# Two groups' scores in one row-tiled session, projections out of the attention's banks, and a re-ordered opening, in a sliding-window attention followed by a SwiGLU block

## The chip, the cores and the metric

One core of one Trainium2 chip. The metric is device time in microseconds (us) of one execution; the trace is taken on one such execution, and its span is 1.6 to 2 us shorter than the device time of that same execution. Engines: PE is TensorE's matmuls, PEld its weight loads, DVE is VectorE, ACT is ScalarE, POOL is GpSimd, SP is the engine whose queue issues all the DMAs here. "Faster" or "slower" needs 2%.

## The reference

Causal attention with a window of 64 positions, 8 batches x 8 heads x 576 positions x 64, then a SwiGLU feed-forward block over 4608 tokens (512 to 1536 to 512):

```python
scores = (1/8) * q @ k.T                  # masked to 0 <= i - j < 64
attn = exp(scores - max); attn = attn / (sum(attn) + 1e-9)
x = (attn @ v) as [4608, 512]
g = x @ w_gate;  h = g * (1 / (1 + exp(-g))) * (x @ w_val)
out = h @ w_out                           # float32 in and out
```

## The kernel before

Tokens go through in 36 groups of 128 (attention) and 9 tiles of 512 (feed-forward). Everything is cast to bf16 and multiplied there. The parts that matter here:

```python
ps_a: 3 banks of PSUM   # scores, products, transposes, in rotation
ps_f: 2 x 2 banks       # gate and value of a feed-forward step
ps_o: 1 bank            # projection, and the warm-up matmuls

def scores(g):                     # one "session": 16 matmuls of 64 rows
    ps = [ps_a.tile(...) for _ in range(2)]
    for b in range(2):
        for p in range(4):
            for a in range(2):
                nc.tensor.matmul(ps[a][:, p, 1 - b], kT[...], qT[...], tile_position=(64 * a, 0))
    for a in range(2):
        act.activation(e, ps[a][:], AF.Exp, scale=0.125)
        dve.tensor_mul(e, e, mask)             # both inputs in SBUF, bf16

def products(g):                   # 16 matmuls of 65 columns, then on DVE:
    ...                            # reciprocal and multiply, twice, from PSUM

def step(t, m):                    # 4 gate and 4 value matmuls, 128x512 each, Tanh on ACT,
    ...                            # then on DVE the two operations of the PREVIOUS step
                                   # ("finish"), which free its gate and value banks

def warm(n):                       # n matmuls of zeros, to keep TensorE active
    for _ in range(n): nc.tensor.matmul(w_ps[:], wz[:, 0:P], wz[:])

# opening: a long fixed list of calls. It loads and transposes k and q, does the
# attention of groups 0 to 11 and the scores of 12, all of tile 0 and the gate/value
# steps of tile 1, while the weights arrive. Then the loop:
for w in range(8, 36):
    t, s = divmod(w, 4)
    step(t, 3 * s)
    products(w + 4)
    ...                            # casts of k, q and v on POOL
    step(t, 3 * s + 1)
    scores(w + 5)
    turn_x1(w + 4)                 # DMA transpose of the group's x, for tile t + 1
    step(t, 3 * s + 2)
    ...                            # DMA transposes of k or q
    project(t - 1, s)              # 12 matmuls 128x512, out by ACT and DMA
    ...                            # next loads
for s in range(4): project(8, s)
```

The softmax here doesn't subtract the row's maximum and nothing guards it: scores larger than these inputs give would overflow.

## Time and profile before

| | before |
|---|---|
| device time, median | 355.39 us (3 runs, 354.25 to 355.47) |
| span of the trace | 352.3 us |
| first feed-forward matmul | 27.32 us |
| start of the loop (first step of tile 2) | 97.63 us |
| last matmul ends | 348.45 us |

The page's busy table and its slices of the span (each digit is a tenth of busy time, or of full clock, in one fortieth of the span; GB/s is what DMA moved):

```profile
PE 336.3 (95%) x2629; PEld 164.3 (47%) x2629; DVE 232.4 (66%) x488; ACT 149.2 (42%) x255; POOL 101.3 (29%) x144
...
PEclk9999999999999999999999999999999999999999
...
GB/s 205 241 283 298 308 248 285 283 203 153 99 169 183 158 164 180 165 158 159 179 152 178 158 171 163 168 151 180 151 181 165 106 74 47 45 60 33 30 60 89
```

PE is busy 95% of the span, but that hides two stages. The loop is bound by PE. Here is one loop step in the timeline of PE (start, duration, what, count; the products between are left out). Durations overlap because matmuls are pipelined, so starts are what to read:

```profile
204.75 1.03 PE L258 MATMUL g_ps<-xT,wg 128*128 128x512 bf16 x4
205.62 1.03 PE L258 MATMUL v_ps<-xT,wv 128*128 128x512 bf16 x4
206.58 0.41 PE L176 MATMUL s_ps<-qT,kT 64*128 64x64 bf16 x16
206.92 1.04 PE L258 MATMUL g_ps<-xT,wg 128*128 128x512 bf16 x4
...
213.45 1.02 PE L258 MATMUL g_ps<-xT,wg 128*128 128x512 bf16 x4
```

Four 128x512 matmuls take 0.865 us from start to start (205.62 minus 204.75, which the lines show rounded), 0.216 each. A step with products and scores takes 213.45 minus 204.75 = 8.70 us, one without both 7.77. The session sits between the value matmuls and the next gate matmuls: 206.92 - 205.62 - 0.865 = 0.43 us. The 16 scores start 14.5 ns apart, so 0.21 us of that is not score work but entering and leaving.

The opening is different. From the durations, its 71.6 us of PE work (24 steps x 1.727, 4 projections x 2.59, 12 products x 0.48, 13 sessions x 0.44, transposes) take 97.6 us. PE's waits between 27 and 98 us, longest first (total us, times, longest), and pieces of the chain of waits in the same stretch (start, us, what):

```profile
PE s_ps L176 <- ACT E L182: 2.5, 2, 2.2
PE tp L141 <- POOL q_fb L110: 1.6, 1, 1.6
PE tp L141 <- DVE k_fb L110: 0.5, 1, 0.5
```

```profile
23.03 3.06 SPq L235
...
30.67 6.22 DMA w_f<-in_moe_w_val_dram
...
53.55 9.70 DMA k_f<-in_k_dram
...
73.58 5.45 DMA q_f<-in_q_dram
```

PE waits little after 27 us; the chain goes through the DMA queue and single loads (a weight block, then k and q).

### The profile page before, as it was taken

To read this page: it belongs to the slowest core of one execution; us is meant where nothing else is said; L and a number is where in the kernel's file an instruction comes from. 1 tells how busy PE (TensorE), PEld (TensorE's weight loads), DVE (VectorE), ACT (ScalarE), POOL (GpSimd) and SP (SyncE) were. 2 spreads that over 40 slices of the span, in tenths; PEclk is the share of its full clock that TensorE was granted. 3 is DMA by queue.
4 is the path that set the end of the run, shared out by engine and by line. 5 is a ranking of instruction groups with operands and counts; after the bars stand their busy time and mean duration, and the time that the engine had idled before them with its cause. 6 is when DMAs were issued, how large, how long until landed. Compare 5 with 4: busy or idle time off the path is not lost.

```text
span 352.3 us, 6919 instructions
## 1 busy us (share of the span) xinstructions
PE 336.3 (95%) x2629; PEld 164.3 (47%) x2629; DVE 232.4 (66%) x488; ACT 149.2 (42%) x255; POOL 101.3 (29%) x144
## 2 busy tenths in 40 slices
PE   8679989997999999999999999999999999999995
PEld 3445544454544444444444444444444444444442
DVE  4778988765786766676667666666666676555510
ACT  2557853649443333333333333333333333333221
POOL 1755445420214324232324151515061310000000
PEclk9999999999999999999999999999999999999999
DMA  8999999997379788989999988888798431110012
GB/s 205 241 283 298 308 248 285 283 203 153 99 169 183 158 164 180 165 158 159 179 152 178 158 171 163 168 151 180 151 181 165 106 74 47 45 60 33 30 60 89
DMA packets 152417, 57.08 MB, mean 162 GB/s; under 512 B 127808, under 2 KB 146240, under 8 KB 152384
## 3 DMA queue, kind: packets, MB, share of 16 engines
q1 hardware_dynamic: 152384, 56.64, 76.1%
q8 instruction: 20, 0.33, 0.4%
q14 instruction: 13, 0.11, 0.1%
HBM read 37.75 MB, written 9.44 MB: 134 GB/s over the span
## 4 chain that ended last, share of the span: by engine, by line
PE 77%; DMA 8%; SPq 8%; DVE 4%; ACT 2%; issue 1%; DVEq 0%; ACTq 0%
PE o_ps L275 24%; PE g_ps L258 22%; PE v_ps L258 21%; SPq L235 3%; DMA k_f<-in_k_dram 3%; PE s_ps L176 3%; PE ao_ps L198 2%; PE ao_ps L202 2%; DMA w_f<-in_moe_w_val_dram 2%; SPq L82 2%; PE w_ps L287 2%; DMA q_f<-in_q_dram 2%; DMA xT<-x_b 1%; SPq L93 1%; DVE hT L270 1%
## 5 line engine op out<-in xcount | busy, mean ns | idle before, releaser
L258 PE MATMUL g_ps<-xT,wg 128*128 128x512 bf16 x432 | 111.1, 380 | 0.5 <-DMA xT<-x_b 0.3
L258 PE MATMUL v_ps<-xT,wv 128*128 128x512 bf16 x432 | 110.9, 379 | 0.1
L275 PE MATMUL o_ps<-wo,hT 128*128 128x512 bf16 x432 | 98.5, 379 | 0.0
L263 ACT ACTIVATE th<-g_ps 128x512 f32<-128x512 f32 x108 | 64.6, 599 | 67.0 <-PE g_ps L258 65.8
L269 DVE SCALAR_TENSOR_TENSOR sg<-th,g_ps 128x512 f32<-128x512 f32 x108 | 73.5, 681 | 15.8 <-ACT th L263 15.7
L270 DVE TENSOR_TENSOR hT<-sg,v_ps 128x512 bf16<-128x512 f32 x108 | 74.3, 688 | 9.4 <-DVE sg L269 0.5
L258 PEld LDWEIGHTS <-wv 128*128 128x128 bf16 x432 | 42.0, 98 | 51.5 <-POOL wv L110 0.6
L275 PEld LDWEIGHTS <-hT 128*128 128x128 bf16 x432 | 42.0, 98 | 50.1
L258 PEld LDWEIGHTS <-wg 128*128 128x128 bf16 x432 | 37.8, 98 | 39.0 <-DMA xT<-x_b 1.7
L183 DVE TENSOR_TENSOR E<-E,mask 128x512 bf16<-128x512 bf16 x72 | 34.9, 492 | 22.1 <-ACT E L182 20.4
L182 ACT ACTIVATE E<-s_ps 128x512 bf16<-128x512 f32 x72 | 39.0, 595 | 18.8 <-PE s_ps L176 18.8
L206 DVE RECIPROCAL r<-ao_ps 128x4 f32<-128x4 f32 x72 | 12.7, 177 | 45.2 <-PE ao_ps L202 45.2
L110 POOL CAST ve<-v_f 64x512 bf16<-64x512 f32 x65 | 40.8, 628 | 4.0
L110 POOL CAST q_fb<-q_f 128x1024 bf16<-128x1024 f32 x12 | 12.5, 1038 | 71.0 <-DMA q_f<-in_q_dram 64.7
L207 DVE TENSOR_TENSOR x_b<-ao_ps,r 128x256 bf16<-128x256 f32 x72 | 30.6, 425 | 2.5
L110 POOL CAST k_fb<-k_f 128x1024 bf16<-128x1024 f32 (+1 forms) x14 | 14.4, 1030 | 61.8 <-DMA k_f<-in_k_dram 53.3
L110 POOL CAST vo<-v_f 128x512 bf16<-128x512 f32 x33 | 20.7, 627 | 37.8 <-DMA v_f<-in_v_dram 34.8
L198 PE MATMUL ao_ps<-ve,E 128*128 128x65 bf16 x288 | 22.8, 193 | 3.1 <-DVE x_b L207 1.2
L198 PEld LDWEIGHTS <-E 128*128 128x128 bf16 x288 | 20.1, 97 | 7.0 <-DVE x_b L207 1.9
L202 PE MATMUL ao_ps<-vo,E 128*128 128x65 bf16 x288 | 22.9, 193 | 0.0
L202 PEld LDWEIGHTS <-E 128*128 128x128 bf16 x288 | 18.9, 97 | 4.2 <-issue 0.5
L176 PEld LDWEIGHTS <-kT 64*128 64x128 bf16 x576 | 11.0, 95 | 19.1 <-issue 16.3
(84 smaller groups left out, 138.4 us busy)
## 6 DMA issues: line engine op xcount, KB each, us to landing
v_f<-in_v_dram SPq DMA_DIRECT2D x32, 256.0 KB, 4.5
q_f<-in_q_dram SPq DMA_DIRECT2D x23, 256.0 KB, 4.5
k_f<-in_k_dram SPq DMA_DIRECT2D x23, 256.0 KB, 4.1
w_f<-in_moe_w_val_dram SPq DMA_DIRECT2D x6, 512.0 KB, 8.0
w_f<-in_moe_w_gate_dram SPq DMA_DIRECT2D x6, 512.0 KB, 7.6
wo_f<-in_moe_w_out_dram SPq DMA_DIRECT2D x6, 512.0 KB, 8.0
k_f<-in_k_dram SPq DMA_DIRECT2D x4, 512.0 KB, 7.4
q_f<-in_q_dram SPq DMA_DIRECT2D x4, 512.0 KB, 6.8
```

The source lines that it names most:

```text
L110: eng.tensor_copy(y, x)
L176: nc.tensor.matmul(ps[a][:, p, 1 - b], kT[g // 2 % KR][y, p, o:o + P], qT[g // 2 % QR][y, p, o:o + 64], tile_position=(64 * a, 0),)
L182: act.activation(e, ps[a][:], AF.Exp, scale=0.125)
L183: dve.tensor_mul(e, e, mk[:].unsqueeze(1).to_broadcast([P, 4, 2, 64]))
L198: nc.tensor.matmul(o_ps[:, i, :], E[:, e + P:e + 2 * P], ve[g % VR][:, y, :], start=True, stop=False,)
L202: nc.tensor.matmul(o_ps[:, i, :], E[:, e:e + P], vo[g % VR][:, y, :], start=False, stop=True,)
L207: dve.tensor_mul(x_b[:, 256 * h:256 * h + 256].rearrange("r (y d) -> r y d", y=4), o_ps[:, :, 0:D], r[:].unsqueeze(2).to_broadcast([P, 4, D]),
L258: nc.tensor.matmul(ps[:, 0:n], w[:, c, P * m:P * m + P], xT[t][:, c, c0:c0 + n], start=(c == 0), stop=(c == 3),)
L263: act.activation(th[:, 0:n], g_ps[:, 0:n], AF.Tanh, scale=0.5)
L269: dve.scalar_tensor_tensor(sg[:, 0:n], th[:, 0:n], 1.0, g_ps[:, 0:n], ALU.add, ALU.mult)
L270: dve.tensor_mul(hT[t][:, m, c0:c0 + n], sg[:, 0:n], v_ps[:, 0:n])
L275: nc.tensor.matmul(o_ps[:], hT[t][:, c, P * s:P * s + P], wo[:, c, :], start=(c == 0), stop=(c == 11),)
```

## The change

The intent: one change of TensorE's tiling mode for two groups instead of for one; four shared banks to hold two groups' scores, won by giving up the projection's own bank; and a new order of the opening, with helpers that can split the cast of v over engines.

```diff
-    ps_a = ... tc.tile_pool(name="ps_a", bufs=3, space=PSUM)
+    ps_a = ... tc.tile_pool(name="ps_a", bufs=4, space=PSUM)
-    ps_o = ... tc.tile_pool(name="ps_o", bufs=1, space=PSUM)
...
 def scores(g):        # the matmuls only
+    sps[g] = ps
+def weigh(g):         # Exp and mask
+    for a, x in enumerate(sps.pop(g)): ...
...
-    def project(t, s, ps=None, tag="o"):    # and warm(): from ps_a now
+    def project(t, s):
...
     (the opening: the same calls in a new order; loads start k1, q0, k0, q1; scores(5), (4), (6)
      in one session before the first step; one step of tile 0 in two halves; scores up to 13)
...
         step(t, 3 * s + 1)
-        if w + 5 < NG:
-            scores(w + 5)
+        if odd:
+            for g in range(w + 5, min(w + 7, NG)):
+                scores(g)
+            if w + 5 < NG:
+                weigh(w + 5)
         turn_x1(w + 4)
         step(t, 3 * s + 2)
+        if odd and w + 6 < NG:
+            weigh(w + 6)
```

The rewriting of `finish` changes no order: it still follows one step behind.

More of the change, by code (lines that the diff above doesn't have):

```diff
@@ L45 @@
     hpool = ctx.enter_context(tc.tile_pool(name="hpool", bufs=2))
-    ps_a = ctx.enter_context(tc.tile_pool(name="ps_a", bufs=3, space=PSUM))
+    ps_a = ctx.enter_context(tc.tile_pool(name="ps_a", bufs=4, space=PSUM))
     ps_f = ctx.enter_context(tc.tile_pool(name="ps_f", bufs=2, space=PSUM))
-    ps_o = ctx.enter_context(tc.tile_pool(name="ps_o", bufs=1, space=PSUM))
     wg = cst.tile([P, 4, DFF], BF16, name="wg")
@@ L150, in turn2, with cast_v @@
             copy(eng, y, x)
-    def cast_v(g, eng, parts=(0, 1, 2)):
+    def cast_v(g, engs):
         x = staged["v_f", g // 2][:, g % 2]
         lo, hi = slice(0, 64), slice(64, P)
-        for i in parts:
-            if i == 0:
-                copy(eng, vo[g % VR][:, :, 0:D], x)
-            if i == 1:
-                copy(eng, ve[g % VR][hi, :, 0:D], x[lo])
-            if i == 2 and g + 1 < NG:
-                copy(eng, ve[(g + 1) % VR][lo, :, 0:D], x[hi])
-    def scores(g):
-        E = Es[g % ER]
-        mk = masks[0]
-        for b in range(2):
-            if (2 * g + b) % 9 == 0:
-                mk = masks[2 - b]
+        engs = engs if isinstance(engs, tuple) else (engs,) * 3
+        z = vo[g % VR]
+        copy(engs[0], z[:, :, 0:D], x)
+        for e, a, b in ((engs[1], ve[g % VR][hi], lo), (engs[2], ve[(g + 1) % VR][lo], hi)):
+            if e is None:
+                dve.tensor_copy(a, z[b])
+            else:
+                copy(e, a[:, :, 0:D], x[b])
+    sps = {}
+    def scores(g):
         ps = [ps_a.tile([P, 4, 2, 64], FP32, name="s_ps", tag="a") for _ in range(2)]
@@ L179, in scores @@
                     )
-        for a in range(2):
+        sps[g] = ps
+    def weigh(g):
+        E = Es[g % ER]
+        mk = masks[0]
+        for b in range(2):
+            if (2 * g + b) % 9 == 0:
+                mk = masks[2 - b]
+        for a, x in enumerate(sps.pop(g)):
             e = E[:, 1:25].rearrange("r (h y) x -> r h y x", y=3)[:, a:H:2, 0:2, :]
-            act.activation(e, ps[a][:], AF.Exp, scale=0.125)
+            act.activation(e, x[:], AF.Exp, scale=0.125)
             dve.tensor_mul(e, e, mk[:].unsqueeze(1).to_broadcast([P, 4, 2, 64]))
@@ L249, with step @@
     hT = {}
-    def gv(t, m, c0=0, n=512):
+    pend = []
+    def step(t, m, c0=0, n=512):
         if t not in hT:
@@ L263, in gv, with finish @@
         act.activation(th[:, 0:n], g_ps[:, 0:n], AF.Tanh, scale=0.5)
-        return g_ps, v_ps, th, t, m, c0, n
-    def finish(state):
-        g_ps, v_ps, th, t, m, c0, n = state
+        pend.append((g_ps, v_ps, th, t, m, c0, n))
+    def finish():
+        g_ps, v_ps, th, t, m, c0, n = pend.pop(0)
         sg = fsb.tile([P, 512], FP32, name="sg", tag="sg")
@@ L270, in finish @@
         dve.tensor_mul(hT[t][:, m, c0:c0 + n], sg[:, 0:n], v_ps[:, 0:n])
-    def project(t, s, ps=None, tag="o"):
-        o_ps = (ps or ps_o).tile([P, 512], FP32, name="o_ps", tag=tag)
+    def project(t, s):
+        o_ps = ps_a.tile([P, 512], FP32, name="o_ps", tag="a")
         for c in range(12):
@@ L284, in warm @@
     def warm(n):
-        w_ps = ps_o.tile([P, 512], FP32, name="w_ps", tag="o")
+        w_ps = ps_a.tile([P, 512], FP32, name="w_ps", tag="a")
         for _ in range(n):
             nc.tensor.matmul(w_ps[:], wz[:, 0:P], wz[:])
-    pend = None
-    def step(t, m, c0=0, n=512):
-        nonlocal pend
-        st = gv(t, m, c0, n)
-        if pend:
-            finish(pend)
-        pend = st
-    def flush():
-        nonlocal pend
-        finish(pend)
-        pend = None
     def begin():
@@ L327 @@
     begin()
+    load(1, k, "k_f")
+    load(0, q, "q_f")
     load(0, k, "k_f")
-    load(0, q, "q_f")
-    load_vg(0)
-    cast_k(0, "k_f", dve)
-    warm(18)
-    turn2(0, "k_f", act)
-    load(1, k, "k_f")
-    keys_before(1)
-    cast_k(0, "q_f", (dve, act))
-    load(1, q, "q_f")
-    load_vg(1)
-    warm(5)
-    turn2(0, "q_f", (dve, act))
-    cast_k(1, "k_f", pool)
-    cast_k(1, "q_f", dve)
+    load(1, q, "q_f")
+    cast_k(0, "k_f", (act, pool))
+    cast_k(0, "q_f", dve)
+    warm(11)
@@ L343 @@
+    turn2(0, "q_f", (dve, act))
+    load_vg(0)
     cast_v(0, pool)
     load_vg(2)
+    cast_v(2, pool)
+    cast_k(1, "k_f", (dve, act))
+    warm(3)
+    turn2(0, "k_f", (dve, act))
+    load_vg(1)
+    cast_k(1, "q_f", dve)
+    turn2(1, "k_f", (dve, act))
+    keys_before(1)
+    warm(1)
+    turn2(1, "q_f", (dve, act))
+    scores(1)
+    weigh(1)
+    load(2, q, "q_f")
+    warm(1)
+    scores(0)
+    weigh(0)
+    warm(1)
+    scores(2)
+    weigh(2)
     cast_v(1, pool)
+    cast_k(2, "q_f", (dve, act))
@@ L346 @@
+    load(3, k, "k_f")
+    warm(5)
+    products(0)
     load(2, k, "k_f")
-    load(2, q, "q_f")
+    scores(3)
+    weigh(3)
+    cast_k(3, "k_f", act)
+    warm(2)
+    turn2(2, "q_f", act)
+    products(1)
+    turn_x(0)
     load_vg(3)
-    cast_v(2, pool)
+    cast_k(2, "k_f", (dve, pool))
+    load(3, q, "q_f")
     warm(2)
-    scores(0)
-    warm(2)
-    scores(1)
-    turn2(1, "k_f", act)
+    products(2)
+    warm(1)
+    turn2(2, "k_f", dve)
+    turn2(3, "k_f", act)
     weights(0, 1)
-    warm(1)
@@ L357 @@
-    turn2(1, "q_f", act)
-    cast_v(3, pool)
-    weights(0, 0)
-    weights(3, 0)
-    products(0)
-    load_vg(4)
-    load(3, k, "k_f")
-    warm(1)
-    products(1)
-    warm(2)
-    scores(2)
-    cast_w(0, 1, pool)
-    cast_k(2, "k_f", act)
-    cast_k(2, "q_f", dve)
-    cast_w(0, 0, pool)
-    warm(2)
-    scores(3)
-    turn_x(0)
-    warm(3)
-    products(2)
-    keys_before(2)
-    weights(3, 1)
-    turn_x(1)
-    products(3)
-    turn2(2, "k_f", (dve, act))
-    turn_x(2)
-    turn2(2, "q_f", (dve, act))
+    weights(0, 0)
@@ L384 @@
+    cast_v(3, pool)
+    load_vg(4)
+    weights(3, 0)
+    turn_x(1)
+    cast_w(0, 0, pool)
+    keys_before(3)
+    weights(3, 1)
+    load_vg(5)
+    cast_k(3, "q_f", dve)
+    warm(1)
+    products(3)
+    keys_before(2)
+    turn_x(2)
+    cast_w(0, 1, dve)
+    load_vg(6)
+    warm(1)
+    turn2(3, "q_f", (dve, act))
+    weights(4, 0)
+    warm(1)
+    turn_x(3)
+    scores(5)
+    weigh(5)
+    scores(4)
+    weigh(4)
+    scores(6)
+    weigh(6)
     cast_v(4, pool)
-    turn_x(3)
-    warm(1)
@@ L387 @@
-    scores(4)
+    weights(4, 1)
     cast_w(3, 0, pool)
-    load_vg(5)
-    cast_v(5, pool)
-    load(3, q, "q_f")
-    step(0, 1)
-    cast_w(3, 1, act)
-    weights(5, 0)
-    cast_w(5, 0, pool)
-    weights(5, 1)
-    load_vg(6)
-    step(0, 0)
-    weights(4, 0)
-    weights(4, 1)
-    cast_k(3, "k_f", dve)
-    weights(2, 0)
-    products(4)
-    load_vg(7)
-    step(0, 7)
-    keys_before(3)
+    step(0, 1)
+    step(0, 0)
+    finish()
+    load_vg(7)
+    weights(5, 0)
+    cast_w(3, 1, act)
@@ L407 @@
+    products(4)
+    step(0, 7)
+    finish()
+    weights(5, 1)
+    weights(2, 0)
+    cast_v(5, pool)
+    cast_w(4, 0, pool)
+    cast_v(6, act)
+    turn_x(4)
+    cast_w(4, 1, pool)
+    products(5)
     weights(2, 1)
-    scores(5)
-    cast_k(3, "q_f", act)
-    turn2(3, "k_f", act)
     step(0, 6)
-    turn2(3, "q_f", act)
-    cast_w(5, 1, dve)
-    products(5)
-    step(0, 11)
-    scores(6)
+    finish()
+    products(6)
+    scores(7)
+    weigh(7)
+    load_vg(8)
+    step(0, 9)
+    finish()
@@ L417 @@
+    turn_x(5)
+    weights(1, 1)
+    cast_v(7, pool)
+    weights(1, 0)
+    turn_x(6)
+    cast_w(5, 1, pool)
+    cast_w(5, 0, act)
+    load_vg(9)
+    load(4, k, "k_f")
+    load(5, k, "k_f")
+    step(0, 8)
+    finish()
+    products(7)
+    step(0, 11)
+    finish()
+    turn_x(7)
+    load(5, q, "q_f")
+    step(0, 10)
+    finish()
+    cast_w(2, 1, dve)
+    cast_w(2, 0, act)
+    step(1, 8)
+    finish()
     load(4, q, "q_f")
-    turn_x(4)
-    cast_v(6, pool)
-    step(0, 10)
     weights_o(2)
-    cast_w(4, 1, act)
@@ L423 @@
-    cast_w(4, 0, pool)
-    turn_x(5)
-    products(6)
-    step(0, 9)
-    weights(1, 0)
-    scores(7)
-    cast_v(7, pool)
-    cast_w(2, 0, act)
-    load_vg(10)
-    weights(1, 1)
-    weights_o(5)
-    weights_o(0)
-    turn_x(6)
-    step(0, 8)
-    cast_w(2, 1, pool)
-    cast_k(4, "q_f", pool)
-    products(7)
-    step(0, 5)
-    load(5, k, "k_f")
-    turn2(4, "q_f", act)
-    cast_v(10, pool)
-    turn_x(7)
-    step(0, 4)
-    step(1, 9)
-    load(4, k, "k_f")
-    step(1, 5)
-    step(1, 8)
@@ L450 @@
-    casts_o(2, pool)
-    casts_o(5, pool)
-    weights_o(4)
-    cast_w(1, 1, dve)
-    step(1, 7)
-    cast_w(1, 0, pool)
-    load_vg(8)
-    weights_o(3)
-    step(1, 2)
-    keys_before(4)
-    load_vg(11)
-    cast_k(4, "k_f", dve)
-    step(0, 2)
-    turn2(4, "k_f", act)
-    weights_o(1)
-    load(5, q, "q_f")
-    casts_o(4, pool)
-    step(0, 3)
-    casts_o(0, act)
-    step(1, 1)
-    cast_k(5, "k_f", (dve, pool))
-    load_vg(9)
-    keys_before(5)
-    scores(8)
-    step(1, 4)
-    cast_v(8, pool)
@@ L476 @@
-    load1(6, k, "k_f")
-    scores(9)
-    casts_o(1, pool)
-    load1(6, q, "q_f")
-    casts_o(3, pool)
-    turn2(5, "k_f", dve)
-    cast_k(5, "q_f", act)
-    load1(7, q, "q_f")
-    cast_k(6, "k_f", pool)
-    project(0, 3)
-    turn1(6, "k_f")
-    turn2(5, "q_f", act)
-    cast_k(6, "q_f", act)
-    products(8)
-    step(1, 3)
-    scores(10)
-    turn1(6, "q_f")
-    turn_x(8)
-    cast_v(9, act)
-    step(1, 6)
-    scores(11)
-    load1(7, k, "k_f")
-    cast_k(7, "k_f", pool)
-    project(0, 1)
@@ L500 @@
-    products(9)
-    step(1, 0)
-    load_vg(12)
-    cast_v(11, act)
-    products(10)
-    load_vg(14)
-    project(0, 2)
-    keys_before(6)
-    scores(12)
-    step(1, 10)
-    products(11)
-    project(0, 0)
-    turn_x(9)
+    step(0, 5)
+    finish()
+    step(0, 4, 0, 256)
+    finish()
+    load_vg(10)
+    weights_o(1)
+    cast_w(1, 0, dve)
+    step(1, 7)
+    finish()
+    cast_v(9, pool)
+    weights_o(3)
+    cast_w(1, 1, dve)
+    step(1, 4)
+    finish()
+    load_vg(11)
+    keys_before(4)
@@ new lines @@
+    cast_k(4, "k_f", pool)
+    step(1, 11)
+    finish()
+    step(1, 2)
+    finish()
+    cast_k(5, "k_f", (dve, pool))
+    turn2(4, "k_f", act)
+    weights_o(4)
+    weights_o(5)
+    step(0, 3)
+    finish()
+    step(1, 9)
+    finish()
+    cast_k(4, "q_f", (dve, pool))
+    weights_o(0)
+    casts_o(2, pool)
+    cast_k(5, "q_f", (dve, pool))
+    load1(6, k, "k_f")
+    step(0, 2)
+    finish()
+    cast_v(8, pool)
+    turn2(4, "q_f", (dve, act))
+    step(0, 4, 256, 256)
+    finish()
@@ new lines @@
+    scores(8)
+    weigh(8)
+    scores(9)
+    weigh(9)
+    step(1, 5)
+    finish()
+    products(8)
+    turn2(5, "q_f", act)
+    keys_before(5)
+    turn2(5, "k_f", act)
+    load1(6, q, "q_f")
+    step(1, 1)
+    finish()
+    products(9)
+    turn_x(8)
+    casts_o(3, pool)
+    step(1, 0)
+    finish()
+    casts_o(1, act)
+    casts_o(5, dve)
+    casts_o(4, dve)
+    cast_k(6, "k_f", dve)
+    casts_o(0, act)
+    cast_v(11, pool)
+    cast_v(10, dve)
+    keys_before(6)
+    cast_k(6, "q_f", (dve, pool))
@@ L513 @@
+    load(7, k, "k_f")
+    scores(10)
+    weigh(10)
+    turn1(6, "k_f")
+    turn1(6, "q_f")
+    load_vg(12)
+    scores(11)
+    weigh(11)
+    step(1, 10)
+    finish()
+    project(0, 3)
+    project(0, 2)
+    products(10)
+    turn_x1(9)
+    project(0, 1)
+    products(11)
+    load_vg(13)
+    load1(8, k, "k_f")
+    step(1, 3)
+    finish()
+    cast_k(7, "k_f", dve)
+    scores(13)
+    weigh(13)
+    scores(12)
+    weigh(12)
+    step(1, 6)
+    finish()
     turn_x(10)
     turn_x(11)
-    turn1(7, "k_f")
@@ L516 @@
-    cast_v(12, dve)
-    step(1, 11)
-    load_vg(13)
-    load1(8, k, "k_f")
+    load1(7, q, "q_f")
+    load_vg(14)
+    turn2(7, "k_f", dve)
+    cast_v(12, pool)
     keys_before(7)
+    project(0, 0)
     for w in range(8, NG):
@@ L526 @@
         step(t, 3 * s)
+        finish()
         if w + 4 < NG:
@@ L535 @@
         step(t, 3 * s + 1)
-        if w + 5 < NG:
-            scores(w + 5)
+        finish()
+        if odd:
[3 more added lines that the diff above has]
+                weigh(w + 5)
         if w + 4 < NG:
@@ L540 @@
         step(t, 3 * s + 2)
+        finish()
+        if odd and w + 6 < NG:
+            weigh(w + 6)
         if odd and n + 4 < NB:
@@ L552 @@
             load1(n + 4, q, "q_f")
-    flush()
+    finish()
     for s in range(4):
-        project(8, s, ps_a, "a")
+        project(8, s)
 _INS = ['q', 'k', 'v', 'moe_w_gate', 'moe_w_val', 'moe_w_out']
```

## The prediction

> **What bounds the kernel now.** The busy table has TensorE (PE) at 95% of a 352.3 us span. The timeline of PE shows the first feed-forward matmul at 27.3 us, the regular loop from 97.6 us and the last matmul ending at 348.45 us.
> - Loop: PE-bound. A 128x512 matmul takes 0.216 us start to start; a loop step without attention 7.77 us, with it 8.70 us. The waits show PE waiting 0.3 us there. DVE is busy 161 of 251 us.
> - Opening: 24 gate/value steps x 1.727, 4 projections x 2.59, 12 products x 0.48, 13 score sessions x 0.44, 12 k/q transposes x 0.46 and 12 x transposes x 0.22 make 71.6 us of useful PE work in 97.6: 26 us lost, about 19.5 before the first feed-forward matmul, 6.5 after. The chain of waits runs from 12.8 to 36.9 us through the DMA issue queue and weight loads, and mostly through loads of k and q from 48 to 79 us: load order paces the opening. The largest PE waits after 27 us are 2.5 us for an Exp (its engine stuck behind a q cast awaiting its load) and 1.6 us for a q cast.
>
> **Row-tiled sessions.** The 16 score matmuls start 14.5 ns apart, but from the last value matmul to the first score is 0.32 us instead of 0.216, and from the last score to the next gate matmul 0.12: about 0.21 us of each 0.44 is entering and leaving. The Trainium skill, "TensorEngine Tiling (Array Packing)", Key Properties, says that changing the tiling mode drains the TensorE; these gaps agree. In the loop 22 groups now share 11 sessions: 11 x 0.21 = 2.3 us, all on the PE chain. Group 13 moves into the opening (0.44 off the loop).
>
> **Banks.** The second pair of score tiles must wait for the product tiles. DVE is done with those 0.7 us earlier in the trace (normalisation ends at 205.9, the session starts at 206.6), so I expect no new wait. The second group's Exp comes after the third step's Tanh, with slack. Giving up the projection's private bank should cost nothing. The finish lag of one step stays; that edit is bookkeeping.
>
> **Opening.** The new order loads 6.0 MiB instead of 5.0 before the first gate/value step can run, so that step should come at about 28 to 28.5 us, but with two more groups of scores and two more transposes behind it. Loads no longer wait long on staging buffers, k4, k5, q4, q5 come well ahead of their use, and the casts that blocked ACT are moved. Summing PE durations in program order against a load rate of 280 to 300 GB/s, I get a loop start near 90 to 91 us; allowing 2 us for waits I don't see, 92 to 93: about 5 us earlier.
>
> **Split casts of v:** no call uses per-part engines; one useless cast at the end costs nothing.
>
> **Sum.** 2.3 + 0.4 + about 5 = 7.6 us off: 355.4 -> 347.8 us. Range 344.0 to 352.5. Faster by over 2% (below 348.3) 0.53, within 2% 0.46, slower 0.01.
>
> **What would show it.** Session: pairs of loop steps take 17.2 us instead of 17.4. Opening: first gate matmul at 27 to 29.5 us, loop at 91 to 94 us, PE waits for Exp and q casts at 50 to 81 us gone; DMA rate no longer dipping to 248 and 203 GB/s near 50 and 75 us.
>
> **What would make it wrong.** The four-bank rotation stalls PE 0.2 us each time, cancelling the sessions' gain; DVE, busy nearly all the time at 30 to 55 us, delays finishes so that gate/value banks are not free; a load lands late and blocks an in-order queue; or the earlier loop meets late transposes by DMA.

## The result, and the profile after

350.5 us median (4 runs, 348.94 to 350.94) against 355.18 (4 runs, 354.25 to 355.47). The ratio is the mean time of one kernel's fast runs over that of the other's of the same rounds, so not quite the ratio of the medians: 0.9865, 95% interval 0.9828 to 0.9902. By the 2% rule that is "same"; it is a clear gain of 1.3%. 350.5 lies inside the predicted range (344.0 to 352.5), 2.7 us above the predicted 347.8, and in the class that was given 0.46 rather than the one given 0.53.

| | before | after | predicted |
|---|---|---|---|
| span of the trace | 352.3 | 348.2 | |
| first feed-forward matmul | 27.32 | 30.70 | 28 to 28.5 |
| start of the loop | 97.63 | 95.97 | 92 to 93 |
| loop start to end of span | 254.7 | 252.2 | 252.0 |

So 1.7 us came from the opening and 2.4 from the loop (about 0.5 of that is group 13's session, which moved to the opening, and 0.3 are waits for DMA that differ from trace to trace; see the experiments).

The page's busy table and slices:

```profile
PE 335.2 (96%) x2634; PEld 167.3 (48%) x2634; DVE 242.7 (70%) x503; ACT 146.6 (42%) x252; POOL 100.5 (29%) x145
...
PEclk9896999999999999999999999999999999999999
...
GB/s 210 241 279 251 336 261 234 323 182 100 226 161 172 176 166 167 168 152 169 181 153 181 168 166 155 179 168 168 166 168 167 107 75 47 53 54 32 30 60 90
```

The clock line is new: slices 2 and 4 show less than full clock. The first of these falls, from about 15.4 to 18.8 us, lies far ahead of the first step, and e3 below, whose program is the same up to there, does not have it. The views that answer to those of before, first the loop in the timeline of PE, an odd step from 208.30 and an even one from 217.24:

```profile
208.30 1.03 PE L266 MATMUL g_ps<-xT,wg 128*128 128x512 bf16 x4
...
211.38 1.03 PE L266 MATMUL v_ps<-xT,wv 128*128 128x512 bf16 x4
212.34 0.64 PE L174 MATMUL s_ps<-qT,kT 64*128 64x64 bf16 x32
212.91 1.04 PE L266 MATMUL g_ps<-xT,wg 128*128 128x512 bf16 x4
...
217.24 1.03 PE L266 MATMUL g_ps<-xT,wg 128*128 128x512 bf16 x4
...
220.31 1.03 PE L266 MATMUL v_ps<-xT,wv 128*128 128x512 bf16 x4
221.25 1.02 PE L266 MATMUL g_ps<-xT,wg 128*128 128x512 bf16 x4
```

The odd step takes 217.24 - 208.30 = 8.94 us, and the even one, without a session, 8.32 (the next starts at 225.56): 17.26 a pair against 17.40. The session of 32 costs 212.91 - 211.38 - 0.865 = 0.67 us, as expected. But in the even step the value matmuls from 220.31 to the next gate matmul at 221.25 take 0.94 instead of 0.865.

The opening's stretch before and after the first step, in the timeline of PE:

```profile
28.70 0.19 PE L174 MATMUL s_ps<-qT,kT 64*128 64x64 bf16 x1 [1.32 <-ACT qT L107]
29.19 0.71 PE L174 MATMUL s_ps<-qT,kT 64*128 64x64 bf16 x16 [0.30 <-ACT xT L227]
...
30.70 1.89 PE L266 MATMUL g_ps<-xT,wg 128*128 128x512 bf16 x4
32.38 1.91 PE L266 MATMUL v_ps<-xT,wv 128*128 128x512 bf16 x4
34.09 1.91 PE L266 MATMUL g_ps<-xT,wg 128*128 128x512 bf16 x4
35.79 1.07 PE L266 MATMUL v_ps<-xT,wv 128*128 128x512 bf16 x4
...
37.18 1.02 PE L266 MATMUL g_ps<-xT,wg 128*128 128x512 bf16 x4
```

The gate and value matmuls at 30.70, 32.38 and 34.09 take 1.7 us per four instead of 0.865: the clock is at half, until about 35.8 us. And the chain of waits ahead of them runs through DVE and ACT:

```profile
26.83 0.60 DVE wv L109
27.43 0.61 DVE qT L109
...
28.07 0.58 ACT qT L107
28.65 0.49 ACT xT L227
29.14 1.00 ACT E L188 x2
...
30.18 0.58 PE s_ps L174 x15
```

A cast of value weights (0.60), the copy of half a transposed q on DVE (0.61), then the other half on ACT (0.58), which did not run beside it, then the copy of x and the Exps.

PE's largest wait between 28 and 97 us (the two others that show are 0.3 us each):

```profile
PE s_ps L174 <- ACT qT L107: 1.7, 2, 1.3
```

The 1.3 us of it, and the two others, lie before the first step. The waits on q casts and on a stuck Exp are gone, as predicted. PE waited for nothing long between 31 and 96 us, and yet that stretch took 65.3 us where PE's own work (the sum as for before, with what the new opening does there) is 62.0.

### The profile page after: what moved, and what is told of

It is laid out like the page before. It is cut to its first block, busy times and chain, and to the rows that moved or that the text cites. A ratio compares the mean times of both kernels' runs of the same rounds, so it can differ in the third digit from the quotient of the medians.

```text
span 348.2 us, 6940 instructions
## 1 busy us (share of the span) xinstructions
PE 335.2 (96%) x2634; PEld 167.3 (48%) x2634; DVE 242.7 (70%) x503; ACT 146.6 (42%) x252; POOL 100.5 (29%) x145
## 4 chain that ended last, share of the span: by engine, by line
PE 89%; DVE 5%; DMA 3%; ACT 1%; issue 0%; SPq 0%; ACTq 0%
PE g_ps L266 27%; PE v_ps L266 26%; PE o_ps L283 26%; PE s_ps L174 2%; PE ao_ps L208 2%; PE ao_ps L204 2%; DMA k_f<-in_k_dram 2%; DMA xT<-x_b 1%; DVE E L189 1%; DVE x_b L213 1%; PE tp L140 1%; DVE kT L109 1%; DVE qT L109 1%; ACT qT L107 1%; PE xtp L226 0%; DVE q_fb L109 0%
## 5 line engine op out<-in xcount | busy, mean ns | idle before, releaser
L266 PE MATMUL g_ps<-xT,wg 128*128 128x512 bf16 (+1 forms) x436 | 112.9, 382 | 0.3 <-DMA xT<-x_b 0.3
L266 PE MATMUL v_ps<-xT,wv 128*128 128x512 bf16 (+1 forms) x436 | 112.0, 379 | 0.0
L271 ACT ACTIVATE th<-g_ps 128x512 f32<-128x512 f32 (+1 forms) x109 | 64.8, 594 | 87.8 <-PE g_ps L266 84.6
L277 DVE SCALAR_TENSOR_TENSOR sg<-th,g_ps 128x512 f32<-128x512 f32 (+1 forms) x109 | 73.6, 675 | 13.4 <-ACT th L271 13.4
L278 DVE TENSOR_TENSOR hT<-sg,v_ps 128x512 bf16<-128x512 f32 (+1 forms) x109 | 74.4, 683 | 9.1
L266 PEld LDWEIGHTS <-wg 128*128 128x128 bf16 x436 | 39.3, 98 | 42.5 <-issue 4.4
L189 DVE TENSOR_TENSOR E<-E,mask 128x512 bf16<-128x512 bf16 x72 | 38.7, 569 | 8.6 <-ACT E L188 7.9
L109 POOL CAST ve<-v_f 64x512 bf16<-64x512 f32 x68 | 43.2, 635 | 4.2
L109 POOL CAST q_fb<-q_f 128x1024 bf16<-128x1024 f32 (+1 forms) x14 | 14.2, 1017 | 86.7 <-DMA q_f<-in_q_dram 51.4
L174 PE MATMUL s_ps<-qT,kT 64*128 64x64 bf16 x576 | 13.5, 194 | 2.9 <-ACT qT L107 2.2
```

Of the source, the lines that this page charges most:

```text
L109: eng.tensor_copy(y, x)
L174: nc.tensor.matmul(ps[a][:, p, 1 - b], kT[g // 2 % KR][y, p, o:o + P], qT[g // 2 % QR][y, p, o:o + 64], tile_position=(64 * a, 0),)
L189: dve.tensor_mul(e, e, mk[:].unsqueeze(1).to_broadcast([P, 4, 2, 64]))
L266: nc.tensor.matmul(ps[:, 0:n], w[:, c, P * m:P * m + P], xT[t][:, c, c0:c0 + n], start=(c == 0), stop=(c == 3),)
L271: act.activation(th[:, 0:n], g_ps[:, 0:n], AF.Tanh, scale=0.5)
L277: dve.scalar_tensor_tensor(sg[:, 0:n], th[:, 0:n], 1.0, g_ps[:, 0:n], ALU.add, ALU.mult)
```

## The experiments

Twelve kernels in three batches, each batch beside the kernel before on its chip (median 353.59, 354.72 and 354.53 us). Ratios are to the kernel before, with 95% intervals. Stretches inside a kernel come from one trace each, so it matters how well they repeat. From the first step to the loop start they repeat well: 65.2 to 65.3 us in the four traces with the opening of the change (after, e2, e4, e5), 64.5 to 64.6 with e3's (e3, e11). The loops do not: six traces with the changed loop (after, e3, e5, e6, e7, e9) run from 251.9 to 253.3 us. All of that spread lies in the odd steps that end a tile of 512 tokens (w = 11, 15, 19, 23), where PE or its weight loads wait for the last DMA transpose of x:

```profile
167.73 1.04 PE L258 MATMUL g_ps<-xT,wg 128*128 128x512 bf16 x4 [0.33 <-DMA xT<-x_b]
```

```profile
165.46 1.04 PE L266 MATMUL g_ps<-xT,wg 128*128 128x512 bf16 x4 [0.32 <-DMA xT<-x_b]
```

(The timeline of PE, before and then after.) Call them tile waits, and count as one what such a step takes beyond the other odd steps (8.93 us; 8.70 in the unpaired loops). In sum (us):

| program of the loop | tile waits | loop start to end without them |
|---|---|---|
| of before: before, e12 | 0.75, 0.52 | 253.9 |
| of before, group 13 in the opening: e2 | 0.72 | 253.4 |
| paired, group 13 in the loop: e1 | 0.46 | 252.3 |
| of the change: after, e3, e5, e6, e7, e9 | 0.48, 0.15, 0.62, 0.41, 1.49, 0.73 | 251.8 |
| late products: e4, e8, e11 | 0.62, 1.42, 0.93 | 251.0 |
| late products, q loads later: e10 | none | 251.0 |

Without the tile waits, loops of the same program agree within 0.05 us. "First step" is the first gate matmul; where its record is missing from the trace (e5 to e8) it is put 0.33 us after the start of the last session part, as in e3.

| run | first step | loop start | loop start to end | device time, median | ratio (95%) |
|---|---|---|---|---|---|
| after | 30.70 | 95.97 | 252.2 | 350.5 | 0.9865 (0.9828 to 0.9902) |
| e1 sessions only | 27.86 | 96.65 | 252.8 | 352.89 | 0.9974 (0.9942 to 1.0006) |
| e2 opening only | 30.84 | 96.10 | 254.1 | 352.02 | 0.9965 (0.9943 to 0.9987) |
| e3 warm-up of 8 | 30.59 | 95.12 | 251.9 | 348.84 | 0.9877 (0.9855 to 0.9898) |
| e4 late products | 30.59 | 95.75 | 251.7 | 349.41 | 0.9890 (0.9865 to 0.9915) |
| e5 after, again | 30.9 | 96.11 | 252.4 | 350.37 | 0.9880 (0.9845 to 0.9915) |
| e6 e3 without 6 masks | 31.26 | 95.77 | 252.2 | 349.17 | 0.9846 (0.9808 to 0.9884) |
| e7 casts moved | 29.54 | 94.74 | 253.3 | 350.29 | 0.9883 (0.9845 to 0.9921) |
| e8 e7 and e4 | 29.35 | 94.38 | 252.4 | 349.32 | 0.9853 (0.9818 to 0.9887) |
| e9 e3 without 20 masks | 31.01 | 94.20 | 252.5 | 347.88 | 0.9818 (0.9779 to 0.9858) |
| e10 e8, q loads later | 30.15 | 94.73 | 251.0 | 347.57 | 0.9819 (0.9784 to 0.9855) |
| e11 e3 and e4 | 30.64 | 95.25 | 252.0 | 349.42 | 0.9862 (0.9827 to 0.9896) |
| e12 before, fewer warm-ups | 27.81 | 97.49 | 254.4 | 354.92 | 1.0021 (0.9975 to 1.0067) |

### e1_sessions_only and e2_opening_only: the two halves of the change

```diff
 e1: the kernel before, with 4 shared banks, scores()/weigh() split, and in the loop
-        scores(w + 5)
+        if w == 8: scores(13); weigh(13)
+        if odd: scores of w + 5 and w + 6, weigh(w + 5)  ...  weigh(w + 6) after the third step
 e2: the changed kernel, and in the loop
-        if odd: (two groups) ...
+        if 13 < w + 5 < NG: scores(w + 5); weigh(w + 5)
```

> The kernel before with its opening in its old order, but the loop's scores paired in one session every second step and the four shared score banks. The changed kernel's trace shows pairs of loop steps of 17.26 us against 17.40, so theory A (sessions save 0.14 us a pair net, 11 pairs) expects 1.5 us off the time before, ratio about 0.9955, even steps of 8.32 us and odd ones of 8.94. Theory B (the four shared banks cost the opening something, since products, transposes and projections there now share them with the warm-up) expects the loop gain but an opening later than 97.6 us, ratio 0.998 to 1.003. Theory C (my prediction's arithmetic, 0.21 us a session with nothing given back) expects 2.3 us, ratio 0.9935.

> The changed kernel with the loop's scores back to one group a step (own session each); opening and banks as changed. Group 13 stays in the opening. If the parts add up, it loses 1.5 us against the changed kernel: about 352.0 us, ratio to before about 0.991, loop step 8.70 us. If pairing was worth the predicted 2.3 us, 352.8 us and 0.993.

Measured: with tile waits taken off, pairing takes 253.9 - 252.3 = 1.6 us off the loop in e1, and e2's loop is 253.4 - 251.8 = 1.6 us longer than that of the change: theory A's 1.5, not the predicted 2.3 (11 pairs of 17.26 us against 17.40 give 1.5). The plain loops differ by 1.9 (e1, 254.7 - 252.8) and 1.9 (e2, 254.1 - 252.2); the 0.3 more is tile waits. e1's opening ended 1 us earlier than before's, so in that execution the shared banks did not cost it. That execution is the second fastest of six, though (351.09 us; four others, without a trace, took 352.6 to 354.3), so theory B is not excluded for those. The clock does not order e1's times (351.09 us at 0.995, 354.28 at 0.994), and its ratio leaves the size open. e2's ratio of 0.9965 is less of a gain than expected (0.991), and its spans, 349.8 to 351.3 us, belong to clocks of 0.983 to 0.995. The two halves' gains, 0.26% and 0.35%, do not add up to 1.2 to 1.35% within what the intervals show; the times alone cannot split the gain, and the loop's length in the traces is the better witness.

### e3_warm8: is it the clock?

```diff
     weights(4, 0)
-    warm(1)
+    warm(8)
     turn_x(3)
```

> The changed kernel with 8 warm-up matmuls instead of 1 before the last transpose ahead of the first feed-forward step, in time in which TensorE waits anyway (26.1 to 28.7 us). Theory A: the granted clock fell to 0.5 from about 28.9 to 35.4 us because TensorE did too little in the stretch before; with the warm-up the clock stays 1.00 there, the first two gate/value steps take 1.73 us each instead of 3.4 and 3.1, and the loop starts 2 to 3 us earlier: about 348.0 us, ratio to before 0.979 to 0.982. Theory B: the clock does not matter because the finishes on VectorE, behind six masks until 33.8 us, hold the gate/value banks anyway: clock 1.00, but the third step still starts at 36 to 37 us and the time stays within 0.5 us of the changed kernel (0.9865). Theory C: the fall of the clock has nothing to do with idle time: it stays at 0.5.

The windows view of PE (window, length, PE busy and instructions, granted clock, DMA share, GB/s), of the changed kernel and then of e3:

```profile
25.50:28.90 3.40, 1.84 (x31) 1.00 1.20 261
30.00:31.50 1.50, 1.31 (x17) 0.50 1.23 292
...
34.50:36.00 1.50, 1.50 (x5) 0.54 1.09 380
```

```profile
25.50:28.90 3.40, 3.07 (x38) 1.00 1.19 241
30.00:36.00 6.00, 5.69 (x53) 1.00 1.03 259
```

PE was busy for 1.84 of the 3.40 us before the clock fell, against 3.07 in e3, where it did not fall. The Trainium skill, "TensorE: Matmul & The Clock Gate", Part 1, says that the clock is throttled by default, that activity releases it, and that the window which judges activity runs freely; the trace agrees on the two clocks (0.50 and 1.00 granted), and no run here shows the window itself. The other traces settle that it was no accident of one execution: all four with one warm-up matmul there (after, e2, e4, e5; PE busy 1.84 to 2.15 us of the 3.40) have the first steps at half clock, and none of the seven with 4 or 8 (e3, e6 to e11; 2.69 to 3.26 us). So theory C fell: too little work on PE ahead of the first step caused the fall. The third step starts at 34.74 instead of 37.18 us, 2.4 us earlier, without the first step moving. But the loop starts only 0.85 us earlier. PE now waits where it did not before; its waits in e3 after 28 us:

```profile
PE g_ps L266 <- DVE sg L277: 1.3, 2, 0.9
```

Theory A holds for the clock and theory B for most of its worth: the half clock had hidden that DVE could not follow. In device time no gain is resolved: e3's ratio is 0.9877, where A expected 0.979 to 0.982 and the changed kernel itself has 0.9865 and, again in e5, 0.9880.

### e4_late_products: the 0.07 us of the even steps

```diff
         step(t, 3 * s)
-        if w + 4 < NG:
+        if odd and w + 4 < NG:
             products(w + 4)
         step(t, 3 * s + 1)
+        if not odd and w + 4 < NG:
+            products(w + 4)
```

> The changed kernel with the products of even loop steps moved behind the second gate/value step, where the score session used to be, so that the finish of the first step is not queued behind their normalisation on VectorE. Theory A: the 0.07 us that even steps lose (8.32 us against a sum of 8.25; gap from value matmul to next gate matmul 0.94 instead of 0.87) is the wait of the third step for the gate bank which that finish frees, hidden behind the session before: even steps become 8.25 us, 12 to 14 of them save 0.8 to 1.0 us, ratio to before about 0.984. Theory B: the gap has another cause (a change of shape on TensorE): it stays and the time is that of the changed kernel, 0.9865.

The timeline of PE for an even step of e4:

```profile
216.54 1.03 PE L266 MATMUL g_ps<-xT,wg 128*128 128x512 bf16 x4
217.41 1.03 PE L266 MATMUL v_ps<-xT,wv 128*128 128x512 bf16 x4
218.27 1.03 PE L266 MATMUL g_ps<-xT,wg 128*128 128x512 bf16 x4
219.13 1.03 PE L266 MATMUL v_ps<-xT,wv 128*128 128x512 bf16 x4
...
220.48 1.03 PE L266 MATMUL g_ps<-xT,wg 128*128 128x512 bf16 x4
```

The second step follows the first at once (218.27 - 217.41 = 0.86), the third comes 1.35 us after the second step's value matmuls began, which is their 0.865 and the products' 0.48, and the even step takes 8.26 us (the next starts at 224.80), so theory A is right about the cause: the gate bank was not free, because the finish that frees it stood behind the products' normalisation on DVE. All twelve even steps of e4 take 8.25 or 8.26 us, and with tile waits taken off its loop is 0.8 us shorter (251.0 against 251.8), as theory A said. With them it is only 0.5 us shorter in these two traces, and the ratio (0.989) is no better than that of the changed kernel.

### e5_after_again: the yardstick

The changed kernel, unedited.

> The changed kernel itself, unedited, as the yardstick of this batch on the same chip as the others. Ratio to before 0.984 to 0.989, as on record; granted clock 0.985 to 0.995 in its profile, with a stretch at half clock between 26 and 36 us.

0.9880 and 350.37 us: the result repeats. Its six granted clocks were 0.985 to 0.993, all below those of e3 (1.0 in four of five runs).

### e6_warm8_nomask and e9_nomask10: is it VectorE?

```diff
 e6 (on e3):
+            if g not in (4, 5, 6):
                 dve.tensor_mul(e, e, mask)
 e9 (on e3):
+            if not 4 <= g <= 13:
                 dve.tensor_mul(e, e, mask)
```

Both results are wrong.

> The 8-warm-up version with the six mask multiplications of groups 4, 5 and 6 left out (a wrong result on purpose), which takes some 4.3 us of VectorE work out of the stretch from 29.7 to 34.0 us. With the warm-up the clock was full but only 0.85 us of the 2.4 us gained at the third step was left at the loop's start. Theory A: that rest is lost because VectorE, busy without a break from 29.7 to about 50 us, sets the pace: without the masks the waits for its finishes near 34 and 43 us go, the third step starts at 34.2 to 34.6 us instead of 34.74, and the loop starts 1.5 to 2.5 us earlier than 95.1. Theory B: what sets the pace later is the load order (casts waiting for k5, q5 or the output weights between 56 and 85 us): the steps at 34 to 50 us move earlier, but the loop starts within 0.5 us of 95.1.

> The 8-warm-up version without the masks of groups 4 to 13 (a wrong result on purpose): 20 multiplications, at least 20 x 0.41 = 8 us of VectorE work, taken out of the whole opening after the first feed-forward step, where leaving out only six gave 1.5 us by 22 us after that step but nothing at the loop's start. Measure: loop start minus first gate matmul; TensorE's own work there is 62.0 us, the 8-warm-up version had 64.5, the one without six masks 64.3. Theory A (VectorE, 96% busy from 30 to 82 us, paces the opening; after the six masks were taken out, others became longer, four masks 3.47 us instead of 2.04, while GpSimd was casting): 62.3 to 63.2 us. Theory B (the order of the loads paces it): 63.9 to 64.6 us again.

(The expectation of e9 quotes 64.3 us for e6, reckoned from a first step whose first record is missing, and a share of 96% for DVE; the right numbers are 64.5 us and, for 30 to 82 us, the shares below.)

e6 looked like theory B: 64.5 us from first step to loop start, as in e3. Along the way it was ahead by 0.9 us at the step with half the columns (21.0 us after the first step against 21.9) and by 1.1 at the transpose of k4, and then lost it all. The loss can be seen in the timeline of DVE, in the four masks of groups 8 and 9, in e3 and then in e6:

```profile
69.44 2.04 DVE L189 TENSOR_TENSOR E<-E,mask 128x512 bf16<-128x512 bf16 x4 [0.35 <-ACT E L188]
```

```profile
69.00 3.47 DVE L190 TENSOR_TENSOR E<-E,mask 128x512 bf16<-128x512 bf16 x4 [0.35 <-ACT E L188]
```

The same four instructions took 2.04 and 3.47 us. GpSimd's casts overlap two of the four in e3 and all four in e6. Over the whole changed kernel, the 43 masks that no GpSimd instruction overlaps take 0.41 to 0.43 us each, and the 29 that one overlaps 0.41 to 1.26; in every other trace, too, no mask without such an overlap takes more than 0.43. The Trainium skill, "SBUF — State Buffer", section "Who interferes with whom", says that a VectorE instruction with two SBUF inputs contends with a GpSimd instruction that reads SBUF, and that the contention is an exclusive lock; the masks have two SBUF inputs and GpSimd's casts read SBUF, and these durations agree. e9, which takes these masks out too, needs 94.20 - 31.01 = 63.2 us, 1.3 less than e3 and 1.2 more than PE's work of 62.0. So theory A holds, at the edge of its range: VectorE paced the stretch, and in e6 the masks of groups 8 and 9 took back in collisions (3.47 us against 2.04) what leaving out 6 had gained (1.1). The remaining 1.2 us stay unassigned.

DVE's busy time from 30 to 82 us, by the windows view, for before, after, e3 and e9:

```profile
30.00:82.00 52.00, 40.73 (x79) 1.00 1.10 263
```

```profile
30.00:82.00 52.00, 46.97 (x95) 0.94 0.99 254
```

```profile
30.00:82.00 52.00, 48.86 (x98) 1.00 1.06 257
```

```profile
30.00:82.00 52.00, 42.53 (x85) 1.00 1.09 260
```

78% before, 90% after at a partly halved clock, 94% with the full clock (e3), 82% without the 20 masks (e9).

### e7_casts_moved and e8_best: the late first step

```diff
+    cast_w(0, 1, pool)
     cast_w(0, 0, pool)
...
-    cast_w(0, 1, dve)
...
-    turn2(3, "q_f", (dve, act))
+    turn2(3, "q_f", act)
-    warm(1)
+    warm(4)
 e8: and the loop of e4
```

> The changed kernel with 4 warm-up matmuls instead of 1, the cast of the first value weights moved from VectorE (0.69 us, straight ahead of the copy of the last q transpose) to GpSimd, and that copy done by ScalarE alone in one piece (1.03 us) instead of in two that ran one after the other (0.61 and 0.58). Theory A: the first gate/value step (30.7 us) was held by the chain cast, copy, copy, x copy, Exp; then qT is ready about 1.2 us earlier and the first step starts at 29.5 to 29.9 us, bounded then by the gate weights' load and cast (landed 28.4, cast 1.04); the loop starts about 0.8 to 1.0 us earlier than with 8 warm-ups (95.1). Theory B: the first step is held by the gate weights already: it starts at 30.4 to 30.7 and nothing is gained beyond the clock.

> The version of the moved casts together with the products of even loop steps behind the second gate/value step. If both parts add up: the loop start of the moved casts (about 94.2 us), and a loop that is 1.0 us shorter than that of the changed kernel (251.6 instead of 252.2 to 252.5 us): about 1.8 to 2.5 us faster than the changed kernel, ratio to before about 0.980 to 0.982.

The first step starts at 29.5 us in e7, as theory A said, 1.1 us earlier than e3's, but only 0.4 us are left at the loop's start (94.74), so the step's lateness was mostly not worth its own size either. (The same opening gave 29.35 and 94.38 us in e8, and 30.15 and 94.73 in e10, whose first step waited 0.48 us for the cast of the gate weights.) And e7's loop is 1.1 us longer than the changed kernel's, all of it in tile waits: PE waits for the x transposes by DMA, 1.0 us in two places, and in e8 0.8 in one:

```profile
164.31 1.04 PE L266 MATMUL g_ps<-xT,wg 128*128 128x512 bf16 x4 [0.82 <-DMA xT<-x_b]
```

e7 is no faster than the changed kernel of its batch (350.29 and 350.37). e8 is, by 1.0 us of median (349.32). Its two parts did not add up as expected.

### e11_warm8_late and e10_best2: where the late products' gain went

```diff
 e11: the opening of e3 with the loop of e4
 e10 (on e8):
         turn_x1(w + 4)
+        if odd and n + 4 < NB:
+            load1(n + 4, q, "q_f")
         step(t, 3 * s + 2)
 ...
-        if not odd and n + 4 < NB:
-            load1(n + 4, q, "q_f")
```

> The changed kernel with 8 warm-up matmuls instead of 1 and the products of even steps behind the second gate/value step, nothing else moved. If the two single edits add up: loop start about 95.1 to 95.6 us, loop 251.5 us, span about 346.5 to 347.0 us, ratio to before about 0.984 and 1.5 to 2 us faster than the changed kernel; if not (0.985 or more) one edit eats the other's gain.

> The version of moved casts and late products, with the loop's loads of q issued after the transpose of the next x tile instead of before it, because in that version the loop lost 0.8 us at the start of a token tile, waiting for the last x transpose by DMA, which took 5.9 us to land while a q load of three pieces was in flight. Theory A (the wait comes from that load being ahead in the queue): no such wait, loop 251.6 us, span about 346.0 us and 0.8 us faster than the version before it. Theory B (the DMA engines, near 0.9 busy in the loop, are simply full): a wait of 0.3 to 1 us remains somewhere in the loop.

e11 missed: 0.9862, and its loop of 252.0 us is as long as e3's (251.9), although its even steps are shorter by 0.07 us each. Its tile waits are 0.93 us against 0.15 in e3 (weight loads waiting for x transposes 1.8 against 0.8), and they eat the gain. That later products make x, and so its transpose, later is a possible reason and not shown: tile waits with early products run from 0.15 to 1.49 us, and with late ones from 0.62 to 1.42 (e4, e8, e11). e10 shows what removes them. With the q load issued behind the x transpose instead of ahead of it, no wait for a transpose is left in the loop, the transposes land after 2.7 us in the median (3.4 in e8), and the loop takes 251.0 us, the shortest of all. In this one trace theory A holds: the queue order, not full DMA engines, made the wait. e10 is the best kernel here: 347.57 us against 349.42 for e11 in the same rounds (its opening differs too), and 0.9819 (0.9784 to 0.9855) of before. e8, from which it differs by that one edit, ran in another batch (0.9853).

### e12_before_cold: the same clock in the kernel before

```diff
 the kernel before, every warm(n) after warm(18) left out
```

> The kernel before without any of its warm-up matmuls after the first 18. Theory A: warm-up matmuls keep the clock up in the opening, and without them TensorE's clock is at half for one or more stretches between 9 and 36 us (mean granted clock 0.98 to 0.99 in the profile), which costs 0.5 to 3 us: 354 to 357 us where before has 353.6 to 354.7. Theory B: the clock falls for other reasons (the chip, the phase of a timer) and the mean clock and the time stay as those of before, 0.994 to 1.0.

The granted clock was 0.976 to 0.985 (before: 0.993 to 1.0), at half from about 12.0 to 15.5 us and from 18.9 to 25.7 us in the profile: theory A for the clock. The price was not resolved: 354.92 against 354.53 us, ratio 1.0021 (0.9975 to 1.0067). In the profiled run the clock was full again before the first step at 27.8 us, so it never met the dense work; that this is why it cost so little is an inference.

## Why the prediction was right or wrong

- **Sessions.** Right in mechanism, mis-sized. The step "11 x 0.21 = 2.3 us, all on the PE chain" gave 1.5 by the steps' lengths (17.26 us a pair against 17.40) and 1.6 by the loops without their tile waits (e1, e2). The mode change does cost what was read (0.67 for a session of 32 is 2 x 0.44 less 0.21), but half of the steps lost 0.07 us to a bank wait that the session had hidden, and e4 shows its cause. "I expect no new wait" looked at the score banks alone, where it was right, and not at the gate bank. That the loop took 252.2 us, so near the predicted 252.0, is in part luck: 0.3 us of its gain are tile waits.
- **Shared banks.** Right, as far as e1's one trace goes, that giving up the projection's bank costs nothing visible.
- **First gate/value step.** "About 28 to 28.5 us" was 30.7. The loads and casts were not what held it, though it was put down to the load order: DVE's queue with one weight cast, and two half copies that ran one after the other, held the last q. Moving them gained 1.1 us in e7's trace, and 0.4 in e10's. I had counted PE and the loads and not DVE and ACT before that step.
- **Opening.** This is the step that failed in size: "loop start near 90 to 91 us; allowing 2 us for waits I don't see, 92 to 93: about 5 us earlier". It was 1.7 us earlier. Summing PE's work in order was right for PE: no long PE wait shows after the first step. What it missed was the half clock (worth 2.4 us at the third step, but 0.85 at the loop's start, e3) and DVE, 90 to 94% busy, whose relief brings 1.3 us (e9). Some 1.2 us stay open. The chain of waits had made me call load order the pace; in the new opening, once the clock is full, VectorE is the only pace that was shown. That the total of 350.5 us still fell inside the range is owed to the range's upper end, 4.7 us above the predicted time, and not to the sum, whose largest term was three times too large.
- **Waits gone, loads free.** Right about the Exp and q casts at 50 to 81 us. The DMA rate still dips (234, 182 and 100 GB/s near 57, 74 and 83 us), so that sign was wrong, and nothing came of it.
- **What would make it wrong** named DVE delaying the finishes, and late DMA transposes once the loop comes earlier. The first happened (e3). The transposes were late in places too, but that an earlier loop made them so is not shown: tile waits took 0.75 us in before already and 0.48 in after; they were largest in e7 and e8 (1.49 and 1.42), but 0.73 in e9, whose loop starts first of all (94.20). It did not name the clock, which the page of before showed at full everywhere.

## What to carry to other kernels

A re-ordered opening must be counted on every engine that works in it, and its idle stretches on TensorE are worth filling with warm-up matmuls: here the first dense work ran at half clock with one of them ahead of it and at full clock with 4 or 8. Check what then comes last; here it was VectorE, and little of the gain was left. A gain of 0.2 us at one point is only a gain if no wait was hidden behind what was removed: compare the step's length with the sum of its parts after the change. When a stage moves earlier, look at the queues in order (casts on VectorE, DMA issues) for the next thing that now comes last. And before two loops are compared by their total length, take off the waits that come and go from trace to trace.

## What the Trainium skill lacked or had wrong

- "TensorEngine Tiling (Array Packing)", Key Properties, says that changing the tiling mode drains TensorE but gives no cost. Here entering and leaving a session of 16 matmuls cost 0.21 us together, and a session of 32 0.67 us against 2 x 0.43 for two of 16.
- "TensorE: Matmul & The Clock Gate", Part 1, puts the return to half clock in its table down to an idle window of about 3.4 us; further on the page knows of falls from frequent short idles, but gives no share of busy time for them. Here it came with PE 54% busy over the 3.4 us before (1.84 us, transposes included) and no single gap above 1.32 us, and it varied from run to run of one kernel (mean clock 0.985 to 0.993 in ten runs). The two granted clocks, full and half, agree, at 0.216 and 0.43 us a 128x512 matmul.
- "SBUF — State Buffer", Who interferes with whom, names the contention that fits here but gives no size for this pair: a two-input bf16 multiply of 128x512 took 0.41 to 0.43 us with no GpSimd instruction beside it, and up to 1.26 us in the changed kernel where a cast overlapped it.
